# Parted loads of k, v and q, tied between the u transposes, and earlier token-mixing weights, in a fused attention and mixer kernel

## Chip, cores and metric

One core of one Trainium2 chip. The metric is the device time of one execution in microseconds (us); lower is better. Each kernel was run several times beside the kernel before on the same chip. A ratio is the mean time of one kernel's runs over the mean of the other's runs of the same rounds, so it is not quite the ratio of the medians that are quoted beside it.

## The reference

Eight batches (B), eight heads (H) of 64, a sequence of 1024. The attention has its keys and values projected to 64 rows; a two-step MLP-mixer follows.

```python
k_proj = einsum('ks,bhsd->bhkd', E, k);  v_proj = einsum('ks,bhsd->bhkd', F, v)
attn   = softmax(q @ k_proj.T / sqrt(64)) @ v_proj
x = attn.transpose(0, 2, 1, 3).reshape(B, S, H * 64)          # (8, 1024, 512)
h = relu(x.T @ w_tok1) @ w_tok2                               # token mixing, 1024 -> 256 -> 1024
u = x + h.T
out = u + relu(u @ w_ch1) @ w_ch2                             # channel mixing, 512 -> 1536 -> 512
```

## The kernel before

A planner in the program orders all work. Each piece is a "job" on one engine with its dependencies and a priority; the planner emits all jobs in one order, and each engine executes its own in that order. The front of a batch (projection of k and v, scores, attention, token mixing, u) is woven between the channel mixing of the batches before it, because channel mixing fills TensorE: its up and down matmuls are 62% of the chain of work in the trace before, where TensorE is busy 49.00 of 49.00 us from 196 to 245 us.

A batch is two blocks of 512 tokens. When a block's u is ready, SyncE issues one DMA transpose into `uT`; VectorE then makes four sums `S` of quarters of `uT`, and TensorE multiplies `uT` and `S` by the channel weights ("up", then "down"):

```python
def s_sums(j):                       # j: block number, two per batch
    St = S_t[j % 2]
    a11, a12, a21, a22 = [quarter(j, sh, dh) for sh in range(2) for dh in range(2)]
    ...
    one(0, a21, a22, add=True)       # each is one VectorE instruction, 128x512
    one(2, a11, a21)
    one(1, St[:, 0], a11, deps=(0,))
    one(3, a12, St[:, 1], deps=(1,))
```

VectorE also multiplies the attention outputs by the softmax reciprocals (`x_sb<-ps,rdn`). The next batch's k, v and q are loaded by GpSimd's queue in one group of six, and "ties" make loads and transposes take turns:

```python
    # in token2, at the end of each block's u
    j = sp(3.5, lambda: nc.sync.dma_start_transpose(out=uT_t[i]..., in_=u_t[b % 2]...), ...)
    if landed[0]:
        tie(j, landed[0])            # every u transpose waits for the last load group
    turned[0] = j
# ... (cut)
def load_batch(b):
    jobs = [load_heads(b, n, hh, H // 2, None) for n in "kvq" for hh in range(0, H, H // 2)]
    for j in jobs if turned[0] else ():
        tie(j, turned[0])            # the group waits for the last transpose
    landed[0] = jobs[-1]
```

A tie is both an edge for the planner and a semaphore wait in the program. The wait is weaker than the comments in the code: it is for one load of the group, which the planner need not place last. In the trace before, the u transpose at 269.21 us runs while packets of GpSimd's queue move until about 274 us. One listing of line numbers helps to read the profiles, since the edits shift them:

| work | before | after | most experiments |
|---|---|---|---|
| loads of k, v, q (GpSimd's queue) | L314 | L315 | L315 |
| u transpose (SyncE's queue) | L649 | L653 | L654 |
| S sums (VectorE) | L671 | L675 | L676 |
| x multiplies (VectorE) | L595 | L599 | L600 |
| kp copies (VectorE) / k transposes (TensorE) | L471 / L492 | L474 / L495 | L475 / L496 |
| attention (TensorE) | L578 | L582 | L583 |
| up / down matmuls (TensorE) | L801 / L896 | L805 / L900 | L807 / L902 |

The softmax here doesn't subtract the row's maximum and nothing guards it: scores larger than these inputs give would overflow.

## Time and profile before

| | before |
|---|---|
| median of the first three runs | 439.78 us (438.99 to 440.23) |
| TensorE idle, 0 to 44 us | 9.05 us |
| TensorE idle, 98 to 245 us | 0.09 us |
| TensorE idle, 245 to 392 us | 3.09 us |

The idle times are window length less PE busy, from the table by stretch that the prediction quotes in part. The remaining waits of TensorE are few and short (engine, line and tile, what it waited for; us in all, times, longest):

```profile
PE ps L555 <- ACT kT L507: 4.7, 4, 1.4
...
PE ps L492 <- DVE kp L471: 0.7, 1, 0.7
PE ps L578 <- DVE x_sb L595: 0.6, 1, 0.6
```

VectorE's x multiplies are named for 0.9 us in all, 0.6 here and 0.3 in a line left out.

### The profile page before, as it was taken

The page shows a single profiled execution, that of the slowest core. Times are in us where ns is not written, and L with a number is a line of the kernel's source. Part 1 is how long each engine was busy: PE and PEld are TensorE (multiplying, and loading weights), DVE is VectorE, ACT ScalarE, POOL GpSimd, SP SyncE. Part 2 cuts the span into 40 slices and gives each one's busy share as a digit, 9 for nine tenths or more (in the row PEclk, how much of TensorE's full clock was granted, in tenths as well). Part 3 has the DMA queues.
Part 4 walks back from the last instruction along what each step waited for, and adds up shares of the span by engine and source line. Part 5 has one row for each costly group of instructions (what it writes and reads, how often), then busy time and mean ns, then how long its engine had stood idle before and what let it go on. Part 6 is the DMA issues. An engine that isn't in the chain of part 4 may idle for free.

```text
span 439.5 us, 9315 instructions
## 1 busy us (share of the span) xinstructions
PE 418.5 (95%) x3736; PEld 338.4 (77%) x3736; DVE 321.0 (73%) x783; ACT 241.1 (55%) x439; POOL 106.2 (24%) x122
## 2 busy tenths in 40 slices
PE   6789999999999999999999999899999999999993
PEld 4468888578778886788778877688768886888883
DVE  3459969678978797779697696778697596966451
ACT  1557786258536754567356654558436663555540
POOL 8442123032301331115021331115112210212212
PEclk9999999999999999999999999999999999999999
DMA  9999979289955899198955899187992811241022
GB/s 167 208 199 207 206 123 195 91 186 167 177 94 152 126 194 172 46 224 149 197 89 120 139 189 203 22 193 140 199 142 47 195 48 49 50 145 61 36 98 95
DMA packets 89516, 60.89 MB, mean 139 GB/s; under 512 B 55681, under 2 KB 84865, under 8 KB 89473
## 3 DMA queue, kind: packets, MB, share of 16 engines
q0 software_dynamic: 30624, 29.36, 42.7%
q1 hardware_dynamic: 58768, 30.68, 29.4%
q8 instruction: 29, 0.48, 0.4%
q10 hardware_dynamic: 80, 0.26, 0.3%
q14 instruction: 15, 0.11, 0.1%
HBM read 59.24 MB, written 16.78 MB: 173 GB/s over the span
## 4 chain that ended last, share of the span: by engine, by line
PE 86%; DVE 7%; ACT 2%; DMA 2%; issue 1%; DVEq 0%; ACTq 0%
PE ps L896 32%; PE ps L801 30%; PE ps L609 6%; PE ps L629 5%; PE ps L555 3%; PE ps L455 3%; PE ps L578 3%; DMA uT<-u 2%; DVE S L671 1%; DVE u L728 1%; PE ps L539 1%; ACT qT L547 1%; PE ps L377 1%; PE ps L689 1%; DVE da L943 1%
## 5 line engine op out<-in xcount | busy, mean ns | idle before, releaser
L896 PEld LDWEIGHTS <-G 128*128 128x128 bf16 x1344 | 130.0, 98 | 24.5 <-issue 5.7
L896 PE MATMUL ps<-wc_sb,G 128*128 128x256 bf16 x768 | 103.8, 273 | 3.9 <-DVE da L943 2.7
L801 PEld LDWEIGHTS <-wc_sb 128*128 128x128 bf16 x768 | 73.6, 98 | 14.3 <-issue 1.6
L823 ACT ACTIVATE G<-ps 128x512 bf16<-128x512 f32 x96 | 57.2, 599 | 39.9 <-PE ps L801 39.6
L896 PE MATMUL ps<-wT,G 128*128 128x256 bf16 x576 | 77.7, 272 | 0.1
L927 POOL TENSOR_TENSOR o<-o,u 128x512 f32<-128x512 f32 x32 | 37.4, 1169 | 130.3 <-ACT o L925 115.2
L801 PEld LDWEIGHTS <-wT 128*128 128x128 bf16 x576 | 55.1, 98 | 11.2 <-issue 2.2
L801 PE MATMUL ps<-uT,wc_sb 128*128 128x256 bf16 x384 | 57.6, 273 | 0.0
L801 PE MATMUL ps<-S,wc_sb 128*128 128x256 bf16 x384 | 57.6, 273 | 0.0
L927 POOL TENSOR_TENSOR db<-db,u 128x512 f32<-128x512 f32 x16 | 18.9, 1182 | 157.5 <-ACT db L925 157.5
L801 PE MATMUL ps<-S,wT 128*128 128x256 bf16 x384 | 54.9, 273 | 0.9 <-ACT G L823 0.7
L640 DVE TENSOR_TENSOR u<-ps,x_sb 128x512 bf16<-128x512 f32 x56 | 35.7, 684 | 22.2 <-PE ps L629 21.7
L595 DVE TENSOR_TENSOR x_sb<-ps,rdn 128x256 bf16<-128x256 f32 x128 | 49.7, 415 | 0.3
L836 DVE TENSOR_TENSOR G<-G 128x512 bf16<-128x512 bf16 x96 | 46.7, 489 | 3.4
L782 DVE CUSTOM_DVE_ANT_0 g<-ps,ub 128x512 bf16<-128x512 f32 x48 | 32.8, 684 | 20.4 <-PE ps L801 20.3
L782 DVE CUSTOM_DVE_ANT_0 G<-ps,ua 128x512 bf16<-128x512 f32 x48 | 32.7, 682 | 18.1 <-ACT ua L829 18.0
L564 ACT ACTIVATE a<-ps 128x512 bf16<-128x512 f32 x64 | 37.1, 600 | 12.4 <-PE ps L555 12.2
L829 ACT COPY ua<-ps 128x512 f32<-128x512 f32 x48 | 28.1, 586 | 24.2 <-PE ps L801 23.6
L829 ACT COPY ub<-ps 128x512 f32<-128x512 f32 x48 | 28.1, 586 | 9.6 <-PE ps L801 9.2
L842 ACT COPY ps<-ps 128x512 f32<-128x512 f32 x48 | 28.3, 589 | 6.9 <-DVE g L782 4.2
L578 PE MATMUL ps<-vb,a 128*128 128x130 bf16 x256 | 30.9, 226 | 0.6 <-DVE x_sb L595 0.6
L629 PE MATMUL ps<-hT_sb,wt_sb 128*128 128x512 bf16 x112 | 29.5, 379 | 0.0
(69 smaller groups left out, 521.7 us busy)
## 6 DMA issues: line engine op xcount, KB each, us to landing
out_dram<-o SPq DMA_DIRECT2D x32, 512.0 KB, 3.6
k_sb<-in_k_dram POOLq DMA_DIRECT2D x14, 512.0 KB, 8.6
v_sb<-in_v_dram POOLq DMA_DIRECT2D x14, 512.0 KB, 13.0
q_sb<-in_q_dram POOLq DMA_DIRECT2D x14, 512.0 KB, 9.9
wc_sb<-in_moe_w_ch_dram POOLq DMA_DIRECT2D x6, 256.0 KB, 12.9
wc_sb<-in_moe_w_ch_dram POOLq DMA_DIRECT2D x4, 384.0 KB, 12.1
k_sb<-in_k_dram POOLq DMA_DIRECT2D x4, 256.0 KB, 6.7
v_sb<-in_v_dram POOLq DMA_DIRECT2D x4, 256.0 KB, 7.2
```

Source lines behind the costliest of these rows:

```text
L564: lambda: nc.scalar.activation(out=a_t[h % 4], in_=bank(bk), func=ACT.Exp, scale=scale),
L578: nc.tensor.matmul(view()[:, 2 * jj : 2 * jj + 2].rearrange("p c d -> p (c d)"), a_t[h % 4][:, j * P : (j + 1) * P], vb[:, h].rearrange("k ...
L595: lambda: nc.vector.tensor_tensor(out=x_sb[:, 4 * half : 4 * half + 4, h * D : (h + 1) * D], in0=view()[:, :, 0:D], in1=rdn[:, :, None].to ...
L629: nc.tensor.matmul(bank(bk), wt2_sb[:, t, si::NSI], hT_sb[:, t, :], start=(t == 0), stop=(t == TC - 1),)
L640: lambda: nc.vector.tensor_add(out=u_t[b % 2][:, si, :], in0=bank(bk), in1=x_sb[:, si, :]),
L782: nc.vector._custom_dve(TENSOR_ADD_SAT, out=out, in0=in0, in1=in1, s0=FMAX, s1=0.0)
L801: nc.tensor.matmul(t[:, c, :], w1_of(n, dd, 2 * m + c), a_of(j, n, dd), start=(n in (1, 7) and c == 0 and dd == 0), stop=(c == 1 and dd == 1),
L823: lambda: nc.scalar.activation(out=G[:, n, cs], in_=view(src), func=ACT.Relu),
L829: 512, lambda: nc.scalar.copy(out=dst, in_=view("y")), writes=[(name, s % 2)],
L836: 512, lambda: f(out=G[:, n, cs], in0=in0, in1=in1), ps=False, reads=deps,
L896: nc.tensor.matmul(view(X_OF[n])[:, t, :], G[:, G_OF[n], cc, t * P : (t + 1) * P], w2_of(n, cc), start=(n in (1, 7) and t == 0 and cc == 0 ...
L927: 512, lambda: nc.gpsimd.tensor_add(out=dst, in0=dst, in1=u_of(sh, dh)),
```

## The change

Its intent: the long group of loads no longer stands between transposes and their readers. k and v go behind the *first* u transpose of a block pair and ahead of the *second*, q goes behind the q transposes, and at the start both token-mixing weights are loaded after the second head pair instead of one before and one after the last. The core of the diff (left out besides what is marked: a guard in the planner for jobs whose readers have no priority yet):

```diff
+LOADS = "01tT23"          # order of the first loads: head pairs 0, 1, both token weights, pairs 2, 3
 # ... the loop over LOADS replaces: pairs 0, 1, 2, wt1, pair 3, wt2 (cut)
-    def q_transpose(due):
+    def q_transpose(b, behind):
 # ... (cut)
+        landed[0] = load_group(b + 1, "q", j) if b + 1 < B else None
 # ... in token2
-            if landed[0]:
+            if i == 0 and landed[0]:
                 tie(j, landed[0])
-            turned[0] = j
+            turned_u[b, i] = j
 # ... in s_sums: S[2] comes first and needs only half of uT
+        one(2, a11, a21)
         one(0, a21, a22, add=True)
-        one(2, a11, a21)
 # ...
-    def load_batch(b):
-        jobs = [load_heads(b, n, hh, H // 2, None) for n in "kvq" for hh in range(0, H, H // 2)]
-        for j in jobs if turned[0] else ():
-            tie(j, turned[0])
-        landed[0] = jobs[-1]
+    def load_group(b, names, behind):
+        jobs = [load_heads(b, n, hh, H // 2, None) for n in names for hh in range(0, H, H // 2)]
+        for j in jobs if behind else ():
+            tie(j, behind)
+        return jobs[-1]
+
+    def load_kv(b):
+        last = load_group(b, "kv", turned_u.get((b - 2, 0)))
+        if (b - 2, 1) in turned_u:
+            tie(turned_u[b - 2, 1], last)      # the second u transpose waits for k and v
 # ... in front: load_kv(b + 1) right after the projection of k and v, load_batch gone (cut)
```

The tie in `load_kv` is called "the gate" below. No arithmetic changes.

More of the change, by code (lines that the diff above doesn't have):

```diff
@@ L77, in plan @@
             if j.prio is None:
-                due = [s.prio for s in j.next]
+                due = [s.prio for s in j.next if s.prio is not None]
                 j.prio = (min(due) if due else 1e9) - j.occ - 0.3
@@ L331 @@
     first = iter(range(-1000, 0))
-    for hp in range(HP):
-        if hp == HP - 1:
-            w1t = moe_w_tok1.rearrange("(p si) t -> p si t", p=P)
+    w1t = moe_w_tok1.rearrange("(p si) t -> p si t", p=P)
+    w2t = moe_w_tok2.rearrange("(tc p) s -> p tc s", p=P)
+    for step in LOADS:
+        if step == "t":
             ld(1.05, dma(wt1_sb, w1t), writes=["wt1"], prio=next(first))
-        for name in "kvq":
-            load_heads(0, name, 2 * hp, 2, next(first))
-    w2t = moe_w_tok2.rearrange("(tc p) s -> p tc s", p=P)
-    ld(1.05, dma(wt2_sb, w2t), writes=["wt2"], prio=next(first))
+        elif step == "T":
+            ld(1.05, dma(wt2_sb, w2t), writes=["wt2"], prio=next(first))
+        else:
+            for name in "kvq":
+                load_heads(0, name, 2 * int(step), 2, next(first))
     w1_v = moe_w_ch1.rearrange("(dc p) (ch c) -> p dc ch c", p=P, ch=2)
@@ L509, in k_transpose @@
         )
-    turned = [None]
+    turned_u = {}
     landed = [None]
-    def q_transpose(due):
+    def q_transpose(b, behind):
         for h in range(0, H, H // 2):
-            before = turned[0]
-            turned[0] = sp(
+            j = sp(
                 3.5,
@@ L523, in q_transpose @@
                 reads=[("q", i) for i in range(h, h + H // 2)],
-                writes=[("qT", i) for i in range(h, h + H // 2)], prio=due,
+                writes=[("qT", i) for i in range(h, h + H // 2)], prio=None,
             )
-            if before:
-                turned[0].deps.add(before)
+            if behind:
+                j.deps.add(behind)
+            behind = j
+        landed[0] = load_group(b + 1, "q", j) if b + 1 < B else None
     def q_transpose_pe(hp, due):
@@ L665, in s_sums @@
         a11, a12, a21, a22 = [quarter(j, sh, dh) for sh in range(2) for dh in range(2)]
-        rd = [("uT", j % 2, n) for n in range(HP)]
         def one(n, in0, in1, add=False, deps=()):
+            rd = [("uT", j % 2, i) for i in range(HP // 2 if n == 2 else HP)]
             f = nc.vector.tensor_add if add else nc.vector.tensor_sub
@@ L997, in front @@
                     unit(0.4, lambda t, hp=hp: q_transpose_pe(hp, t))
+        if b + 1 < B:
+            unit(0.0, lambda t: load_kv(b + 1))
+        if b == 1:
+            unit(0.0, lambda t: load_group(2, "q", None))
         unit(0.4, lambda t: scores(0, t))
@@ L1004, in front @@
                 unit(0.25, lambda t, h=h, half=half: attend(h, half, t))
-        if b + 1 < B:
-            unit(0.0, lambda t: load_batch(b + 1))
         for n in range(TC):
@@ L1028 @@
             if b > 0:
-                q_transpose(None)
+                q_transpose(b + 1, turned_u.get((b - 1, 1)))
             front(b + 1, at - 62, at - 14)
```

## The prediction

> **What bounds the kernel now.** I read four views in this order: the page, the table of busy time by stretch, the timelines of TensorE, VectorE and GpSimd in the first 45 us, and the chain of waits in order of time.
>
> The page says that TensorE is the bound:
>
> ```profile
> PE 418.5 (95%) x3736; PEld 338.4 (77%) x3736; DVE 321.0 (73%) x783; ACT 241.1 (55%) x439; POOL 106.2 (24%) x122
> PE   6789999999999999999999999899999999999993
> DVE  3459969678978797779697696778697596966451
> PE 86%; DVE 7%; ACT 2%; DMA 2%; issue 1%; DVEq 0%; ACTq 0%
> ```
>
> The DVE row is quoted for its start: VectorE is above 90% only in a few slices, two of them (33 to 55 us) straight after the start. Which stretch has TensorE idle time to win is in the table by stretch (window, its length, then busy time of each engine):
>
> ```profile
> 0.00:44.00 44.00, 34.95 (x373) 26.46 (x374) 24.63 (x78) 22.27 (x45) 23.00 (x38) 1.00 1.19 195
> 44.00:98.00 54.00, 52.52 (x485) 41.68 (x485) 43.60 (x108) 32.70 (x59) 11.46 (x12) 1.00 0.87 158
> 196.00:245.00 49.00, 49.00 (x428) 39.55 (x426) 38.20 (x94) 28.14 (x51) 11.04 (x13) 1.00 0.78 149
> 245.00:294.00 49.00, 47.63 (x414) 38.06 (x412) 35.84 (x87) 26.72 (x49) 10.86 (x12) 1.00 0.78 141
> 294.00:343.00 49.00, 48.27 (x421) 38.81 (x419) 38.42 (x95) 27.62 (x51) 11.67 (x12) 1.00 0.80 143
> 343.00:392.00 49.00, 48.01 (x415) 39.62 (x413) 37.00 (x92) 27.02 (x49) 7.01 (x6) 1.00 0.35 94
> ```
>
> Window length less PE busy: 9.05 us idle in the first 44 us, 1.48 to 98 us, none at 196 to 245, then 1.37 + 0.73 + 0.99 = 3.09 us from 245 to 392. The rest of the idle time is the tail, which the change leaves as it is. So two purses are within reach: the start, and 3.1 us in the later batches (plus some of the 1.48).
>
> At the start TensorE waits for chains of small copies, and it is slow:
>
> ```profile
> 18.15 1.03 PE L555 MATMUL ps<-qT,kT 128*128 128x512 bf16 x2 [1.17 <-ACT kT L507]
> ...
> 22.97 0.61 PE L555 MATMUL ps<-qT,kT 128*128 128x512 bf16 x2 [0.78 <-ACT kT L507]
> ...
> 29.66 0.61 PE L555 MATMUL ps<-qT,kT 128*128 128x512 bf16 x2 [1.39 <-ACT kT L507]
> ```
>
> The same two matmuls take 1.03 us before 20 us and 0.61 us after 22 us. The loads stream on GpSimd's queue; each issue waits for the eighth load before it:
>
> ```profile
> 19.39 0.74 POOL L314 DMA_DIRECT2D wc_sb<-in_moe_w_ch_dram  x1 [1.72 <-DMA wt_sb<-in_moe_w_tok_dram]
> ...
> 26.71 0.77 POOL L314 DMA_DIRECT2D wc_sb<-in_moe_w_ch_dram  x1 [1.64 <-DMA wt_sb<-in_moe_w_tok_dram]
> ```
>
> So the first token weight lands at 19.3 us and the second at 26.7 us. A load of a head pair (256 KB) takes 1.3 us of that stream. In the later batches the chain shows what the 3.1 us are:
>
> ```profile
> 269.21 7.15 DMA uT<-u
> 276.39 1.11 DVE S L671
> ```
>
> The u transpose lands after 7.15 us (the median of its issues is 4.6) while the next batch's loads are still arriving, and the sums S that the next block needs come late.
>
> [...]
>
> **The change part by part.** No arithmetic is added or removed: the built program has the same 7444 rows on TensorE. It is all order.
>
> *1. Later batches.* Before, all six loads of a batch (k, v, q, 512 KB each, about 2.6 us of stream, so 15.4 us) form one group between the q transposes and the next u transpose. Now k and v (10.2 us) go between the two u transposes of a block pair, and q (5.1 us) after the q transposes. The first u transpose, whose S sums gate the next block, is no longer behind the end of a 15 us group; only the second waits for k and v, and it has a whole block, half of the 49 us window, to do it in. The built order also spreads the token-mixing matmuls singly among the others, where before they stood in clumps. I expect 7.15 to fall back to about 4.5 us, and 2.0 to 3.0 of the 3.1 us to go: -2.5 us. From 44 to 98 us I expect nothing on balance, as the order there is new too.
>
> *2. The start.* Up to score pair 1 at 18.15 us nothing changes: both kernels load pairs 0 and 1 first. Then both token weights (512 KB, 2.4 us each) come before pair 2. They land at about 15.5 and 18 us, v of pair 2 at 20.5 instead of 15.6, v of pair 3 at 24.3 instead of 21.9. By the end of these loads the same bytes have passed, so the channel weights land as before (the last of the first six at about 35 us). TensorE can now do token mixing of pairs 0 and 1 instead of waiting. Walking the built order with durations of the trace (x multiplies 0.36, reciprocals 0.12, u additions 0.62, sums and weight differences 0.34, warm 128-column matmuls 0.056 us):
> - token 1 of pair 0, cold, to 20.7; attention pair 1 to 21.6; token 2 of pair 0 to about 22.7; token 1 of pair 1 to 24.2; transposes to 24.9; k and v projection of pair 2 from 24.9 (before: 19.1), of pair 3 from 29.1 (before: 25.8). Their loads have landed by then: transfers are not what holds it.
> - score of pair 3 about 32.6 (before 29.66), after the same chain of copies on ScalarE.
> - VectorE from then on is one queue: both early S sums and the kp copies 1.2, attention pair 2 1.9, four weight differences 1.35, attention pair 3 1.9, u of pair 2 1.25, five weight differences 1.7, u of pair 3 1.25. From 29.2, with small gaps, that ends near 40.7 us. Before, the last u addition ends at 36.74 + 1.88 = 38.6.
> - Against that, 12 up-matmuls are done by then instead of 8 (4 x 0.109 = 0.4 us), eight weight differences that stood after 39 us are out of the way, and S[2], moved ahead, lets product 7 start on pairs 0 and 1 alone.
> Net: 2.1 later, less 0.4 and about 0.5 of stalls saved in the up phase, about +1 us. My walk may be off by 2 us; the ready work on TensorE may hide more. I take +0.3.
>
> Sum: -2.5 + 0.3 = -2.2 us, that is 437.6 us. As a change of this kind is rarely kept when it loses the start, I lean to 437.0.
>
> **The rivals.**
> - *The start gains.* If TensorE, filled with token mixing, is dense from 18 us, up to 4 of the 9.05 us idle go, and with part 1 the time is about 432 to 433. For: waits of 1.2 + 0.8 + 1.4 us stand just before scores. Against: those waits are on ScalarE's chain qT, kT, which stays in each pair, and VectorE is above 90% from 33 to 55 us in both orders.
> - *VectorE holds the start back.* Strict order puts weight differences, which wait for channel weights (35 us), ahead of the last u additions. Then the start loses 2 to 3 us and the whole is 439 to 441.
> - *A new wait in the later batches.* GpSimd's queue also does the output additions; a load there that waits for a transpose holds those up, then stores and o buffers. Against: it is 24% busy, and three o buffers stand ready. It would cost 1 to 3 us: 438 to 441.
> - *The transfers were hidden anyway.* Stretches 98 to 245 have next to no idle time under the old grouping, so part 1 may give only 1 us: 438.5.
>
> **Range and chances.** The gain available is 3.1 later plus at most some 4 at the start, 7 us in all, less than the 8.8 us that 2% is; only an earlier warm clock could add. The loss is bounded by the start, 3 us, and new waits, 3 us. Eight times in ten: 432.5 to 441.0. Faster by over 2% 0.07, within 2% 0.91, slower 0.02.
>
> **What would show each step right or wrong.** Part 1: PE busy in stretches of 49 us from 245 on at 48.7 or more, and the u transpose no longer in the chain with 7 us; if idle time there stays at 3 us, step 1 is wrong. Part 2: the last u addition of batch 0 near 40.7 us and the k and v projection of pair 3 near 29 us; if the last u addition ends before 38 us, the start gains and my VectorE walk is wrong. If TensorE shows waits for o or db behind GpSimd, the third rival holds. If the pair of scores that takes 1.03 us falls to 0.61 much before 21 us, the clock has moved, which I do not count on.

## More of the kernel before

For the second block of a batch, the u transpose and its first sums look like this; the first line is from SyncE's queue, the second from VectorE's timeline (start, length, what; in brackets idle time just before and what ended it):

```profile
235.26 1.89 SPq L649 DMA_TRANSPOSE uT<-u  x1
```

```profile
240.26 0.75 DVE L671 TENSOR_TENSOR S<-uT 128x512 bf16<-128x512 bf16 x2
```

The sums start 5.0 us after the transpose was issued and have no idle time of VectorE ahead of them. When they reach the head of the queue, their data is there.

## The result, and the profile after

| | before | after |
|---|---|---|
| median, same chip (4 runs each) | 440.00 us | 451.61 us |
| range | 438.99 to 443.09 | 451.17 to 453.12 |
| ratio | | 1.0258, 95% interval 1.0202 to 1.0314 |

The kernel is 11.6 us slower by the medians. The table by stretch of the kernel after (window, length, busy time of PE, PEld, DVE, ACT and POOL with instruction counts, granted clock, DMA share, GB/s):

```profile
0.00:44.00 44.00, 33.55 (x368) 25.28 (x369) 26.36 (x82) 21.50 (x44) 23.00 (x38) 0.88 1.19 195
...
98.00:147.00 49.00, 46.53 (x403) 37.10 (x401) 38.10 (x88) 27.11 (x50) 11.02 (x12) 1.00 1.14 200
...
196.00:245.00 49.00, 46.59 (x391) 36.86 (x389) 34.67 (x80) 25.83 (x46) 11.43 (x12) 0.97 0.65 125
245.00:294.00 49.00, 46.21 (x387) 36.45 (x385) 34.35 (x88) 24.22 (x44) 9.53 (x10) 0.97 0.63 130
```

Against before (34.95, 48.98, 49.00 and 47.63 us of PE in these four stretches) the start lost 1.4 us of TensorE work, and 98 to 147, 196 to 245 and 245 to 294 us lost 2.45, 2.41 and 1.42 us; in two of them the granted clock is 0.97, not 1.00. Of the eight stretches only 44 to 98 us (53.05 after 52.52) and the last (48.83 after 48.01) gained. Busy time flatters here, since a matmul at half clock is busy for longer (below, 1.01 against 0.60 us for four).

The 0.88 in the first line is no loss against the 1.00 of before: the score pair that the prediction quotes takes 1.03 or 1.04 us before 20 us in both kernels, and the trace before has no clock record ahead of 22.01 us. The kernel after had the full clock from 7.2 to 10.6 us (granted 1.00, then 0.50 to 20.8 us), so its first 52 matmuls were busy for 8.01 us instead of 8.90. That is some 0.9 of the 1.4 us, and not lost work.

The chain of waits (before: PE 86%, DMA 2%) and the waits of TensorE and VectorE say through what:

```profile
PE 79%; DMA 8%; DVE 8%; ACT 2%; issue 2%; DVEq 0%; ACTq 0%
```

```profile
PE ps L582 <- DVE x_sb L599: 4.5, 4, 2.7
...
PE ps L805 <- DVE x_sb L599: 2.4, 1, 2.4
PE ps L495 <- DVE kp L474: 1.7, 2, 1.3
```

```profile
DVE S L675 <- DMA uT<-u: 11.4, 7, 3.4
```

TensorE now waits for the x multiplies and the kp copies, and VectorE waits 11.4 us in all for the u transpose (before: 1.5 us, once). One such place, in order of time. GpSimd's queue issues the loads of k and v of a later batch:

```profile
183.14 0.76 POOL L315 DMA_DIRECT2D v_sb<-in_v_dram  x1
...
189.50 0.79 POOL L315 DMA_DIRECT2D v_sb<-in_v_dram  x1
```

The second u transpose of the batch, which must wait for the last of these to land, on SyncE's queue:

```profile
198.85 1.77 SPq L653 DMA_TRANSPOSE uT<-u  x1
```

VectorE:

```profile
203.26 0.43 DVE L675 TENSOR_TENSOR S<-uT 128x512 bf16<-128x512 bf16 x1 [1.93 <-DMA uT<-u]
...
203.72 1.29 DVE L675 TENSOR_TENSOR S<-S,uT 128x512 bf16<-128x512 bf16 x1
204.93 0.41 DVE L599 TENSOR_TENSOR x_sb<-ps,rdn 128x256 bf16<-128x256 f32 x1
```

TensorE:

```profile
202.71 0.28 PE L582 MATMUL ps<-vb,a 128*128 128x130 bf16 x2
205.40 1.01 PE L805 MATMUL ps<-uT,wc_sb 128*128 128x256 bf16 x4 [2.41 <-DVE x_sb L599]
...
209.11 0.60 PE L805 MATMUL ps<-uT,wc_sb 128*128 128x256 bf16 x4
```

The last load of v is issued at 189.50, the transpose at 198.85 us. VectorE reaches the first S sum at 201.3 us (203.26 less the bracket's 1.93), finds `uT` missing, and stands still. The x multiplies that come after it in VectorE's order are late by at least as much, and TensorE, which needs a PSUM bank back from them, stops for 2.41 us. A second delay adds to this: the second sum takes 1.29 us. GpSimd's output addition runs from 203.58 to 204.72 us, and in the traces before and after the 109 sums that meet no such addition take 0.39 to 0.43 us; every longer one, up to 1.38 us, overlaps with one. Counting the up matmuls block by block through the trace, TensorE does not need a later second block's transpose and sums until some 14 us after the sums begin (block 9: they begin at 257.7 us, the block's first up matmul runs at 272.2 us and the first that reads a sum at 274.8 us). So nobody needed the sums yet; they held up others only by their place in VectorE's order.

The last of TensorE's lines tell a second cost. Four up matmuls take 1.01 us just after the stall, and 0.60 us at 209 us. The table by stretch with short windows:

```profile
205.00:208.60 3.60, 3.20 (x17) 2.34 (x17) 2.40 (x9) 1.17 (x2) 0.00 (x0) 0.53 0.82 157
208.60:211.00 2.40, 2.40 (x27) 2.17 (x25) 2.09 (x7) 0.60 (x1) 0.66 (x1) 1.00 0.00 0
```

For 3.4 us the granted clock is half (0.50 from 205.2 to 208.5 us), which costs another 1.7 us by estimate, half of that time. The same pair of stall and half clock follows at 255.8 to 263 us (2.65 us idle, then a clock of 0.51 from 259.7 to 263.2 us); at 131 to 135 us there are two stalls, 1.31 and 0.79 us, and at 310 us one of 1.32 us, without a fall of the clock (1.00 from 126 to 137 and from 306 to 316 us). An account, in part estimated, of the profiled spans (449.7 less 439.5, 10.2 us): stalls 1.31 + 0.79 + 2.41 + 2.65 + 1.32 = 8.5 us; two falls of the clock, 6.8 us at half speed, 3.4 us; the start some 0.5 to 1 us; less the stalls of before from 280 to 382 us that are gone, 0.71 + 0.61 + 0.73 + 0.55 + 0.44 = 3.0 us. That makes 9.4 to 9.9 of 10.2 us.

### The profile page after: what moved, and what is told of

It is laid out like the page before. It is cut to its first block, busy times and chain, and to the rows that moved or that the text cites.

```text
span 449.7 us, 9336 instructions
## 1 busy us (share of the span) xinstructions
PE 421.4 (94%) x3736; PEld 338.6 (75%) x3736; DVE 320.4 (71%) x783; ACT 242.7 (54%) x439; POOL 105.3 (23%) x122
## 4 chain that ended last, share of the span: by engine, by line
PE 79%; DMA 8%; DVE 8%; ACT 2%; issue 2%; DVEq 0%; ACTq 0%
PE ps L805 29%; PE ps L900 29%; DMA uT<-u 8%; PE ps L613 5%; PE ps L633 5%; PE ps L458 3%; PE ps L582 3%; PE ps L559 3%; DVE x_sb L599 1%; DVE S L675 1%; ACT qT L551 1%; DVE u L732 1%; PE ps L380 1%; DVE wT L419 1%; PE ps L543 1%
## 5 line engine op out<-in xcount | busy, mean ns | idle before, releaser
L900 PE MATMUL ps<-wc_sb,G 128*128 128x256 bf16 x768 | 105.3, 275 | 2.4 <-DVE da L947 1.6
L805 PE MATMUL ps<-uT,wc_sb 128*128 128x256 bf16 x384 | 58.6, 276 | 3.3 <-DVE x_sb L599 2.4
L599 DVE TENSOR_TENSOR x_sb<-ps,rdn 128x256 bf16<-128x256 f32 x128 | 51.1, 416 | 0.9
L644 DVE TENSOR_TENSOR u<-ps,x_sb 128x512 bf16<-128x512 f32 x56 | 38.0, 686 | 11.6 <-PE ps L633 10.0
L840 DVE TENSOR_TENSOR G<-G 128x512 bf16<-128x512 bf16 x96 | 43.6, 456 | 3.3
L582 PE MATMUL ps<-vb,a 128*128 128x130 bf16 x256 | 32.0, 226 | 5.2 <-DVE x_sb L599 4.5
L633 PE MATMUL ps<-hT_sb,wt_sb 128*128 128x512 bf16 x112 | 32.7, 380 | 0.0
```

Of the source, the lines that this page charges most:

```text
L582: nc.tensor.matmul(view()[:, 2 * jj : 2 * jj + 2].rearrange("p c d -> p (c d)"), a_t[h % 4][:, j * P : (j + 1) * P], vb[:, h].rearrange("k ...
L599: lambda: nc.vector.tensor_tensor(out=x_sb[:, 4 * half : 4 * half + 4, h * D : (h + 1) * D], in0=view()[:, :, 0:D], in1=rdn[:, :, None].to ...
L633: nc.tensor.matmul(bank(bk), wt2_sb[:, t, si::NSI], hT_sb[:, t, :], start=(t == 0), stop=(t == TC - 1),)
L644: lambda: nc.vector.tensor_add(out=u_t[b % 2][:, si, :], in0=bank(bk), in1=x_sb[:, si, :]),
L805: nc.tensor.matmul(t[:, c, :], w1_of(n, dd, 2 * m + c), a_of(j, n, dd), start=(n in (1, 7) and c == 0 and dd == 0), stop=(c == 1 and dd == 1),
L840: 512, lambda: f(out=G[:, n, cs], in0=in0, in1=in1), ps=False, reads=deps,
```

## The experiments

Theory A: the gate makes the second u transpose late, and the late transpose stalls VectorE. Its rival B: the new start, with its other timing, is what costs. C, formed when neither had been enough: late transfers would be harmless, were it not for the place of the sums in VectorE's order. Sixteen kernels ran; all were correct but one, which is named.

**1. The gate's wait removed.** The order on all engines stays; only the semaphore wait goes. The data stay right, since the transpose reads nothing that the loads write.

```diff
+            ungated.add(turned_u[b - 2, 1])          # in load_kv
-        if j in tied and tied[j] is not shown:
+        if j in tied and tied[j] is not shown and j not in ungated:
```

> The changed kernel with one semaphore wait taken away: the second u transpose of each batch no longer waits for the landing of k and v. The order of every engine's instructions is unchanged and no data depends on the wait. Theory A (the second u transpose comes late because of this tie; VectorE then stands at the S sums that wait for it, the x multiplies behind them come late, and TensorE runs out of banks): the transpose is issued about 7 us earlier (191 instead of 198.9 us in the fourth batch), VectorE's wait of S for uT falls from 11.4 us in total to below 5 us, no drop of the clock after 44 us, and the time falls from 451.6 to 441 to 446 us. Rival B (the start or the new order of TensorE lost the time): the time stays at 450 to 452 us.

Measured: 444.45 us (442.07 to 444.77), ratio 1.0089 [1.0055, 1.0123]. That takes away about 7 of the 11.6 us. VectorE's wait for the transposes falls, not to nothing:

```profile
DVE S L676 <- DMA uT<-u: 6.3, 5, 2.1
```

and at 131 us the stall is still there, now with the clock falling behind it (six down matmuls take 1.44 us where 0.81 is usual):

```profile
132.68 0.41 PE L496 MATMUL ps<-ident,kp 64*128 64x64 bf16 x8 [0.98 <-DVE kp L475]
133.87 1.44 PE L901 MATMUL ps<-wc_sb,G 128*128 128x256 bf16 x6 [0.79 <-DVE da L948]
```

Without the gate the second transposes run beside the loads and land slowly: the one of the fourth batch is issued at 191.9 us and lands after 10.6 us, at 202.5; in the kernel after it is issued at 198.9 and lands after 4.4 us, at 203.3. Theory A has the larger share, but is not the whole.

**2. The new start alone**, in the kernel before: `LOADS = "01tT23"` with its loop, and S[2] first.

> The kernel before with only the start of the change: both token weights loaded after head pair 1, and S[2] moved ahead. The ties of the later batches are the old ones. Theory A: the start costs only what the traces show of it, about +1 us: 439 to 443 us. Rival B (the start carries the loss, for instance by the clock's drop between 10 and 21 us): 447 us or more.

Measured: 440.99 us (439.47 to 441.5), ratio 1.0012 [0.999, 1.0035], about 0.5 us. Its timeline has the projection of head pair 3 begin here:

```profile
29.05 0.24 PE L458 MATMUL ps<-k_sb,ET_sb 128*64 128x128 bf16 x1
```

The prediction walked to 29.1 us. The interval allows -0.4 to +1.5 us, so the start costs little, if anything.

**3. The old start in the kernel after**: `LOADS = "012t3T"`.

> The changed kernel with the old order of the first loads, all else as changed. Theory A: the stalls of the later batches stay, so 449 to 452 us. Rival B (the start carries the loss): 440 to 443 us.

Measured: 457.74 us (455.66 to 459.48), ratio 1.0407 [1.0368, 1.0446]: slower than the kernel after, where 449 to 452 us had been expected. The expectation missed, but theory B falls with kernels 2 and 3: the new start costs little alone, and without it the loss grows. The planner's whole order moves with the start, and VectorE's wait for u transposes grew from 11.4 to 18.2 us. Why these waits come out longer with this order was not taken apart further.

**4. The four k and v loads emitted together.** In the kernel after, the last v load stands behind an output addition on GpSimd (183.14 to 189.50 us above). If that hold-up is why the gate opens late, closing the gap should help.

```diff
+    for g in groups:                                  # g: the four k and v loads of a batch
+        g = sorted(g, key=plan.index)
+        for n, j in enumerate(g[1:], 1):
+            plan.remove(j)
+            plan.insert(plan.index(g[0]) + n, j)
```

> The changed kernel, all ties kept, but the four loads of k and v of a batch are put together on GpSimd's queue; before, the last one stood behind an output addition that waits for ScalarE. Theory A, narrower form (the tie is harmful only because the last v load is held up on GpSimd's queue, issued at 189.5 instead of about 184 us in the fourth batch): the load lands about 5 us earlier, the second u transpose with it, VectorE's wait of S for uT falls below 4 us, and the time is 440 to 444 us. If the length of the k and v transfers alone makes the transpose late, the time stays above 448 us.

Measured: a wrong result (relative error 0.31) and 464.2 us. In batch 2 the edit moved a v load ahead of the projection that still had to read the old v. Its time says nothing.

**5. The same, only from batch 3 on** (`if len(jobs) == 4 and b > 2`).

> As e4_regroup, mended: the first group (batch 2, whose v is still being read) is left as it was, so the result must be correct. All ties kept; from batch 3 on the four loads of k and v stand together on GpSimd's queue. Narrow theory (the tie hurts only because the last v load is held up behind an output addition): 440 to 445 us and VectorE's wait of S for uT below 5 us. Otherwise (the length of the k and v transfers themselves makes the second transpose late): above 448 us.

Measured: correct, 453.94 us (453.56 to 455.79), ratio 1.0325 [1.0294, 1.0356]. The v load is issued at 182.5 instead of 189.5 us, yet the transpose behind it still starts at 198.6 us, and VectorE's waits for transposes are no shorter, 12.9 us. GpSimd's hold-up is not the cause; the expectation's alternative, the length of the k and v transfers themselves, fits, but was not tested alone.

**6. Kernel 1, and the q loads placed behind the next first u transpose**, to clear 131 us.

```diff
-        landed[0] = load_group(b + 1, "q", j) if b + 1 < B else None
+        landed[0] = load_group(b + 1, "q", turned_u.get((b - 1, 0), j)) if b + 1 < B else None
```

> e1_no_gate with one more change: the q loads of a batch are tied behind the first u transpose that comes next, so the two are not in flight together. In e1_no_gate the first u transpose of batch 2 is issued together with a q load and lands after 10 to 11 us, the k projection's copies behind its S sums on VectorE come late, TensorE waits and its clock drops at 134 us. If that collision is the cause of what e1_no_gate still loses there: the landing falls to below 6 us, the drop at 134 us goes, and the time is 440 to 443 us. If not: 444 us as before.

Measured: 449.0 us (448.1 to 450.75), ratio 1.0209 [1.0175, 1.0243]. Missed. The stall at 131 us did go, but the planner moved the later q loads next to k and v, the second transposes beside them landed after 12.7 to 13.5 us (kernel 1: 10.2 to 11.0), and stalls of 2.3, 2.2 and 2.9 us opened at 151, 205 and 258 us. A wait moved from one place to three others.

**7. The kernel after with no tie's wait at all**, order unchanged (`if False and j in tied ...`).

> The changed kernel with the same order of every engine, but none of the ties' semaphore waits; only waits for data are left. If the ties themselves are all that costs: 438 to 442 us. If they also protect transposes from sharing the engines with loads: 443 us or more, with u transposes that land after 7 to 11 us.

Measured: 450.81 us (448.09 to 453.75), ratio 1.0244 [1.0181, 1.0308]. Nearly as slow, by another road. TensorE's timeline:

```profile
96.86 1.01 PE L805 MATMUL ps<-uT,wc_sb 128*128 128x256 bf16 x4 [6.20 <-DMA uT<-u]
```

A first u transpose, for which TensorE itself was waiting, ran among the loads, landed after 13.3 us (kernel 1: 7.5), and TensorE stood still for 6.2 us. Kernel 1 differs only in keeping the other ties and is 6.4 us faster. So those do protect something; of the ties, the gate of the second transpose is the one shown to do harm.

**8. The kernel before with no tie's wait.**

> The kernel before with none of the ties' waits and the same order. Theory A holds the old ties for harmless, as each batch has one group of loads ahead of the first transpose: 439 to 441 us. If they protect the transposes: 443 us or more.

Measured: 440.21 us (438.68 to 442.2), ratio 1.001 [0.9994, 1.0026]. In the old order the ties held nothing back.

**9. The kernel after, gate and all, with the S sums of second blocks 14 VectorE instructions later** (still ahead of their first reader). This is theory C alone: the transfers are as late as before, only the place on VectorE changes; the order of the other engines is unchanged.

```diff
+    for blk, s in reversed(sums):
+        k = ((14 if blk % 2 else 0) if blk > 1 else 0)
+        if k:
+            to = spot[on_dve[min(rank[s] + k, len(on_dve) - 1)]] + 0.5
+            put[s] = min(to, min(put[x] for x in s.next) - 0.01)
+    plan.sort(key=lambda j: (put[j], spot[j]))
```

> The changed kernel, all ties and transfers kept; only on VectorE, the four S sums of each second block (from batch 1 on) stand 14 VectorE instructions later, still ahead of the matmuls that read them. Theory C (what costs is not that the second transpose is late for TensorE, which reads its sums some 14 us after, but that VectorE's strict order has the sums so early that the x multiplies behind them wait): VectorE's wait of S for uT falls from 11.4 us to below 5 us, TensorE's waits for x_sb (4.5 + 2.4 us) fall below 1 us, no clock drop at 205 and 260 us, and the time falls to 440 to 444 us. If the late transposes themselves starve TensorE: it stays above 448 us.

Measured: 442.68 us (440.68 to 444.28, 19 runs), ratio 1.0053 [1.0038, 1.0069]: 8.9 of the 11.6 us are gone. VectorE at the place shown above:

```profile
202.46 0.42 DVE L600 TENSOR_TENSOR x_sb<-ps,rdn 128x256 bf16<-128x256 f32 x1
...
206.42 0.41 DVE L676 TENSOR_TENSOR S<-uT 128x512 bf16<-128x512 bf16 x1
```

and the short windows for it:

```profile
203.00:205.00 2.00, 2.00 (x23) 1.81 (x22) 1.38 (x4) 1.79 (x4) 0.89 (x1) 1.00 1.12 207
205.00:208.60 3.60, 3.55 (x34) 2.87 (x33) 3.42 (x12) 1.33 (x3) 0.26 (x1) 1.00 1.30 162
```

The multiply that followed the stall at 204.93 us runs at 202.46, the first sum comes only at 206.42 and no longer waits, TensorE is busy throughout (2.00 of 2.00 us, where it had nothing) and the clock stays at 1.00. The transfer is no earlier (issued at 199.89 us, in the kernel after at 198.85). Theory C is confirmed: the late transfer costs nothing here when nothing urgent stands behind its reader in VectorE's queue.

**10. The same, and the first blocks' sums 8 places later too.**

> As e9_s_later, and the S sums of each first block up to 8 VectorE instructions later too, so that the copies of the k projection at 130 us no longer stand behind sums that wait for a transpose. Theory C: another 1 to 2 us less than e9_s_later: 438 to 442 us. If the sums of the first block are needed at once by TensorE: no gain or a loss against e9_s_later.

Measured: 447.42 us (445.93 to 447.91), ratio 1.0156 [1.0131, 1.0181]. Missed. TensorE waits for sums themselves:

```profile
PE ps L807 <- DVE S L676: 3.4, 6, 0.9
```

Of these 3.4 us, 2.3 stand in kernel 9 too. New is 1.1 us at block 2, whose sums had a reader only 2 us behind them. From the third batch on the readers of first blocks' sums are 10 us or more away; there the move opened two stalls of 0.3 us in each of four batches, before a down matmul that waits for `da` and a score that waits for `a`. The rest was not taken apart.

**11. The kernel before with both moves**, and **12. kernel 1 (no gate) with both moves.**

> The kernel before with the same moves of the S sums (14 and 8 places). Its stalls at 280 and 327 us stand behind S sums that wait for a transpose, so by theory C it gains up to 2 us: 437.5 to 440 us. If the kernel before has no such blocking worth the name: 440 us.

> e1_no_gate with the same moves of the S sums as e10_s_later_both. If both cures are for the same wait, it is no better than e10_s_later_both: 438 to 442 us. If the late landing beside loads still hurts: 442 us or more.

Measured: 448.15 us (446.99 to 448.73), ratio 1.0177, and 447.78 us (445.84 to 448.16), ratio 1.0164 [1.0139, 1.019]. Both missed, kernel 12 with the same waits as kernel 10. In kernel 11 TensorE waits only 1.4 us for sums; why it lost 8 us is open. Kernels 10 and 12 differ only by the gate and are equal within 0.4 us, so with the sums out of the way the gate itself costs nothing measurable.

**13. and 14. Kernel 9 with the move limited to blocks 5 to 11, and to 7, 9 and 11**, to learn what the remaining 2.7 us are. (The expectation of 14 puts a half clock behind the stall at 310 us too; the kernel after shows none there, its granted clock is 1.00 from 306 to 316 us.)

```diff
-        k = ((14 if blk % 2 else 0) if blk > 1 else 0)
+        k = 14 if blk % 2 and 5 <= blk <= 11 else 0       # 13;  7 <= blk <= 11 in 14
```

> The changed kernel with the S sums of the second blocks 14 places later on VectorE only for blocks 5, 7, 9 and 11 (the run before had 3, 13 and 15 too). If the move itself costs something where no load delays the transpose, TensorE's wait of 0.9 us for the sums at 115 us goes and so do the small waits in the last batch: 440 to 441.5 us, ratio 0.998 to 1.004. If the rest of the loss lies in the start and in the q loads, it stays at 442 to 443 us, ratio 1.005.

> The same with blocks 7, 9 and 11 alone, the three at which TensorE stopped with a clock at half speed behind it (205, 260 and 310 us). If those three stalls are the whole matter of the sums, it equals the run with blocks 5 to 11 within 0.5 us: 440 to 441.5 us. If block 5 had a hidden lag too, it is 1 to 2 us slower than that run.

Measured: 439.80 us (438.0 to 443.75, 22 runs), ratio 0.9997 [0.998, 1.0014], and 440.09 us (438.5 to 443.88, 22 runs), ratio 1.0003 [0.9987, 1.002]. The kernels are level with before. So the moves of blocks 3, 13 and 15 had themselves cost the 2.7 us: kernel 9's trace has TensorE waiting 0.92 + 0.46 + 0.15 us for block 3's sums at 115 to 122 us, and 1.13 us at 352 us for an x multiply that now stands behind block 13's. And it takes no more than three groups of four VectorE instructions, put 14 places later, to win the 11.6 us back.

**15. Kernel 14, and the two q loads of batch 4 wait for the first u transpose of batch 2** instead of running beside it; the order is the same, one wait is moved.

```diff
+    for q in q_jobs[4]:
+        put[q] = max(put[q], put[turned_u[2, 0]] + 0.1)
+        tied[q] = turned_u[2, 0]
```

> The run before (sums of blocks 7, 9 and 11 later) with one wait moved: the two q loads of batch 4 wait for the first u transpose of batch 2 to land, instead of running beside it; the order on every engine is the same. If the shared time is what the stretch from 98 to 147 us loses, that transpose lands after about 4 to 5 us instead of 10, VectorE's wait of 2.37 us for it at 130.7 us and TensorE's of 1.15 and 0.79 us at 134 us go, and the time is 437.5 to 439 us, ratio 0.994 to 0.998. If the q loads, now later, only push the stall on to the k and v loads and the second u transpose, it stays at 440 us or goes above.

Measured: 442.88 us (441.96 to 443.97), ratio 1.0084 [1.0062, 1.0105]. The first half of the expectation holds, and the time goes the other way. In kernel 14 the first u transpose of batch 2 was issued at 120.48 us, beside a q load at 120.56, and its sums, for which VectorE stood idle for 2.37 us, could start only at 130.72; with the q loads held back it is issued at 117.89 us, and its sums start at 125.67 without a wait. The stretch from 98 to 147 us rises to 48.30 us (kernel 14: 46.44), and the next block shows what the change itself had shown: VectorE, then TensorE,

```profile
150.50 1.10 DVE L676 TENSOR_TENSOR S<-uT 128x512 bf16<-128x512 bf16 x1 [2.56 <-DMA uT<-u]
```

```profile
152.45 0.38 PE L560 MATMUL ps<-qT,kT 128*128 128x512 bf16 x1 [2.54 <-DVE x_sb L600]
```

Block 5's sums had not been moved in kernel 14.

**16. Both: the q loads wait, and blocks 5 to 11 are moved.**

> The run before with block 5's sums moved 14 places later too (blocks 5, 7, 9, 11). If VectorE's order is the whole matter, TensorE's wait of 2.5 us at 153 us and the clock's fall after it go, the stretch from 147 to 196 us comes to 48.5 us or more, and the time is 437 to 438.5 us, ratio 0.993 to 0.998. If the stall moves on, some later stretch loses 2 us and the time stays above 440 us.

Measured: 439.36 us (437.38 to 440.08, 22 runs), ratio 0.997 [0.9956, 0.9985]. It beats both kernels, before by 0.3%: small, but with an interval that leaves 1 out. The ratio is within what was expected, the median 0.9 us above the range. Its table by stretch:

```profile
98.00:147.00 49.00, 48.34 (x420) 38.70 (x419) 39.82 (x93) 28.47 (x52) 11.20 (x12) 1.00 1.06 199
...
245.00:294.00 49.00, 49.00 (x427) 39.37 (x426) 37.72 (x93) 28.25 (x51) 11.42 (x12) 1.00 0.77 146
294.00:343.00 49.00, 49.00 (x428) 39.41 (x427) 37.22 (x92) 27.84 (x51) 6.92 (x6) 1.00 0.48 106
343.00:392.00 49.00, 48.83 (x424) 40.91 (x423) 37.52 (x88) 25.94 (x47) 7.00 (x6) 1.00 0.24 65
```

From 245 to 392 us TensorE is busy 49.00 + 49.00 + 48.83 = 146.83 us, before 143.91: 2.9 us gained, the sum that the prediction's first step had named. Some of it is given back earlier: from 98 to 196 us TensorE is busy 0.87 us less (48.34 + 48.70 against 48.98 + 48.93). Up to 98 us it is busy 0.96 us less (33.49 + 53.02 against 34.95 + 52.52), but 0.9 of that is the first 52 matmuls, which as in the kernel after met the full clock (8.01 instead of 8.90 us).

## Why the prediction was wrong

**Step 1 failed, in one clause.** It says of the gate that "only the second waits for k and v, and it has a whole block, half of the 49 us window, to do it in". At best that is the time until TensorE reads the sums. What sets the time allowed is the strict order of VectorE: the sums stand where the planner put them, and the x multiplies and kp copies behind them wait too. VectorE gave the transpose about 2.5 us after its issue (198.85 to 201.33 us), not half a window, and it landed after 4.4. The prediction cited this strict order for the start and did not apply it here. Kernel 9 shows it: transfers untouched, sums moved, 8.9 us back; with kernels 13 and 14 it is all of the loss.

**The mechanism and size of the gain were right, and hidden.** The first u transposes no longer meet the end of a long group: from 225 us on they land after 4.2 to 5.0 us (before: 4.6 to 7.2). Before's five stalls from 280 to 382 us, 3.0 us, are gone already in the kernel after, and kernel 16 keeps 2.9 us in its last three stretches. The kernel after lost them several times over.

**A term was missing.** The prediction counted on an unchanged clock. In the kernel after both stalls over 2.4 us were followed by 3.4 us at half clock, by estimate 1.7 us more for each. The length of the gaps alone does not decide it: in kernel 1 the half speed came after two of 0.98 and 0.79 us with 0.4 us of work between them (1.44 us for six down matmuls, above), while after 1.31 and 0.79 us at 132 to 135 us in the kernel after, and 1.15 and 0.79 us in kernel 14, the granted clock stayed at 1.00. What does decide it was not shown.

**The bound on the loss was wrong.** "New waits, 3 us" is less than a single one of the large stalls with its fall of the clock (2.41 + 1.7 us). There were stalls at four places, with two clock falls: 11.6 us.

**Step 2 was right.** Predicted +0.3 us (its walk said about +1); kernel 2 measured some +0.5, not told apart from zero. The projection of pair 3 was walked to "near 29 us" and began at 29.05 (kernel after: 28.57). The last u addition of batch 0, walked to 40.7 us, ended at 40.2 (39.7; before: 38.6), so VectorE does end the start later, by less than was walked.

**The rivals.** "A new wait in the later batches" was right in kind. It named GpSimd's queue, and VectorE's was the one that stood still; kernel 5 cleared GpSimd's and was no faster; its sign, waits for o or db behind GpSimd, is not among TensorE's costly waits. The sign that the prediction set for step 1, the u transpose out of the chain, came out reversed: from 2% to 8%. "The transfers were hidden anyway" was half right: between 98 and 245 us nothing was to be won, and something was to be lost.

**Still open:** why the old start makes the kernel after slower still (kernel 3), why the kernel before loses 8 us with both moves (kernel 11), and whether the 0.87 us that kernel 16 gives back from 98 to 196 us can be had.

## What to carry to other kernels

Before delaying a transfer, look up where its first reader stands in its engine's order, not when the result is needed in the end: here the sums of block 9, first read at 274.8 us, held VectorE up for 3.36 us until 257.68 us, and the x multiplies behind them and then TensorE, idle for 2.65 us, waited with them. The profile does not name such a reader at once: it put 6.9 us of TensorE's waits down to the x multiplies, which were not slow themselves (416 ns in the mean, 415 before). If a transfer must come later, move its reader back in the queue with it, and only as far as its own reader allows (14 places were right for blocks 5 to 11 and too many for block 3; 8 were too many for block 2). And look at the granted clock behind a TensorE stall before counting it by its length: here the half clock behind those of 2.41 and 2.65 us added an estimated 1.7 us to each.
